# Fifteen blocks of one batch per tile: a retention kernel's loads without blocks of the next batch

## The chip, the cores and the metric

The kernel runs on one core of one Trainium2 chip. The metric is device time in microseconds (us) for one execution. The engines are called by the names that the profile uses: PE is TensorE's matmuls, PEld its weight loads, DVE is VectorE, ACT is ScalarE, POOL is GpSimd, SP is SyncE. SP and POOL issue the DMAs.

## The reference, cut to what matters

A retention layer (attention with a decaying mask and no softmax) over 8 batches, 8 heads, 576 tokens and 64 features per head is followed by a mixer: a low-rank step along the tokens and a two-layer perceptron along the 512 channels.

```python
# retention: q, k, v are (8, 8, 576, 64)
scores = (1 / sqrt(64)) * q @ k.transpose(0, 1, 3, 2)
gamma  = 1 - 2.0 ** (-5.0 - arange(8))
Dmat   = where(rel >= 0, gamma[:, None, None] ** rel, 0.0)   # rel = i - j
x      = (scores * Dmat) @ v                                  # then (8, 576, 512)
# mixer: U (576, 32), V (32, 576), w_ch1 (512, 2048), w_ch2 (2048, 512)
u   = x + (x.T @ U @ V).T          # along the tokens of each batch
out = u + relu(u @ w_ch1) @ w_ch2
```

All inputs and the output are float32. The kernel computes in bfloat16, and the loads that POOL issues convert on the way.

## The kernel before, in words

**Tiles.** The 8 x 576 = 4,608 rows of u are cut into nine tiles of 512 rows (`NT`), `j` = 0 to 8. Each tile is one pass of the perceptron (16 column blocks of the first product, then the second product). A batch of 576 tokens is a little longer than a tile, so tile `j` needs u of batch `j - 1` or earlier and of the first part of batch `j`, and the attention and the low-rank step of batch `j + 1` are done while PE works on tile `j`. u lies in a ring of 16 blocks of 128 rows (`ring["u"]`, and transposed `ring["uT"]`).

**Order.** The order of each engine's instructions is written out in the program. In the loop at line 1352, each tile has a list of steps with a number each, and a step goes into the program ahead of the perceptron's unit of that number. Every engine and every queue takes its instructions in this order.

**The loads.** q, k and v of a batch are each read as five blocks of 128 tokens by 8 heads (`load_block`); 576 is four and a half times 128, so one of the five is a half block (the last one in an even batch, the first in an odd batch). That makes fifteen blocks: twelve whole ones and three halves. POOL issues them. Batches 0 to 2 are read in another way, batch 3 ahead of the loop, and the loop reads batches 4 to 7, which is what the change is about. In tile `j` = 2 to 5, `wait_for_turns(j)` lets POOL wait until u of batch `j` has been transposed, and then POOL issues loads for batch `j + 2`, with `load_for_turns` at line 305: for the pairs of blocks (0, 1), (2, 3) and (4) first q and then k, and after them v. Three sets of k and v buffers (`k_sets`, `v_sets`, by batch modulo 3) and two of q are used in turn.

**Blocks ahead.** The table `ahead = {4: 0, 5: 1, 6: 2, 7: 3}` says how many of the first blocks of k and v of a batch were already read one tile earlier. Behind the loads of batch `j + 2` and the clearing of the unused half blocks (`clear_pads`), tile `j` reads those blocks of batch `j + 3`, with `load_batch` at line 316. So the tiles read:

| tile | blocks of its own batch | blocks of the next batch |
|---|---|---|
| 2 | 15 of batch 4 | k and v block 0 of batch 5 |
| 3 | 13 of batch 5 | k and v blocks 0 and 1 of batch 6 |
| 4 | 11 of batch 6 | k and v blocks 0 to 2 of batch 7 |
| 5 | 9 of batch 7 | none |

**What reads the loads.** In the same tile `j`, SP issues six DMA transposes for batch `j + 2` (`turn_by_dma`, line 478): for each pair of blocks one of q and one of k, into `qT_all` and `kT_all` (for every other batch these are the buffers `qz` and `kvT`). Behind them on SP stand the transposes of u of batch `j + 1` into `uT_t`, and stores of finished output. ACT scales v in eight instructions, one for each head (`scale_head`, line 294), at the end of tile `j`. In tile `j + 1` PE takes all of this: the products of k and v that make the states (`pss`), the scores (`sc`), and the first products of the perceptron for tile `j + 1`, which read `uT_t`.

Of the kernel before, what the change touches and what calls it, by code (L numbers as in the profile page):

```python
# [67 lines left out]
def kernel(  # L68
# [23 lines left out]
    NB = (S + P - 1) // P  # L92
    HALF = S - (NB - 1) * P
    SP = NB * P
    NHP = H // 2
# [13 lines left out]
    def rows_of(b, m):  # L109
        if b % 2 == 0:  # L110
            return (0, HALF) if m == NB - 1 else (0, P)
        return (HALF, P) if m == 0 else (0, P)

    def token_of(b, m):
        return m * P if b % 2 == 0 else m * P - HALF
# [24 lines left out]
    NRUNS = 3  # L140
    NTURN = 3
    NQ = 2
    q_raw = [consts.tile([P, NR_COLS], BF16, name=f"q_all{i}") for i in range(NQ)]
# [8 lines left out]
    def in_runs(x):  # L152
        return x[0:NR, :].rearrange("p (h i d) -> p h i d", h=H, i=RUN)
# [4 lines left out]
    NSET = 3  # L158
    k_sets = [consts.tile([P, NB, H, D], BF16, name=f"k_all{i}") for i in range(NSET)]
    v_sets = [consts.tile([P, NB, H, D], BF16, name=f"v_all{i}") for i in range(NSET)]  # L160
# [47 lines left out]
    def load_block(dst, src, b, m):  # L208
        lo, hi = rows_of(b, m)
        t0 = max(token_of(b, m), 0)  # L210
        pool.dma_start(
            out=dst[lo:hi, m, :, :],
            in_=src[b, :, t0:t0 + hi - lo, :].rearrange("h s d -> s h d"),
        )

    def load_runs(dst, src, b, hp):

        h = slice(2 * hp, 2 * hp + 2)
        pool.dma_start(
            out=dst[:, h, :, :].rearrange("p h i d -> p h (i d)"),  # L220
            in_=src[b, h, :, :].rearrange("h (p i) d -> p h (i d)", i=RUN),
        )
# [71 lines left out]
    def scale_head(b, h):  # L294

        x = v_sets[b % NSET][:, :, h, :]
        act.activation(out=x, in_=x, func=AF.Copy, scale=vs64[:, h:h + 1])


    def clear_pads(b):  # L300
        m, pad = (NB - 1, slice(HALF, P)) if b % 2 == 0 else (0, slice(0, HALF))
        for x in (k_sets, v_sets):
            pool.memset(x[b % NSET][pad, m, :, :], 0.0)

    def load_for_turns(b, first=0):

        for c in range(0, NB, 2):
            pair = range(c, min(c + 2, NB))
            load_q(b, pair)
            for m in pair:  # L310
                if m >= first:
                    load_block(k_sets[b % NSET], k, b, m)
        for m in range(first, NB):
            load_block(v_sets[b % NSET], v, b, m)

    def load_batch(b, blocks=range(NB)):

        if b < NRUNS:
            for hp in range(NHP):
                load_runs(in_runs(q_raw[b % NQ]), q, b, hp)  # L320
            for x, src in ((k_sets, k), (v_sets, v)):
                for m in blocks:
                    load_block(x[b % NSET], src, b, m)
            return
        for m in blocks:
            load_block(k_sets[b % NSET], k, b, m)
            load_block(v_sets[b % NSET], v, b, m)

    def load_q(b, blocks):
        for m in blocks:  # L330
            load_block(in_blocks(q_raw[b % NQ]), q, b, m)

    def wait_for_turns(b):

        for a, n in in_ring(chunks_of(b)):
            pool.tensor_copy(out=landed[:, 0:n], in_=ring["uT"][:, a:a + n, 0, 0])
# [247 lines left out]
    def attention_steps(b, at, gap, at_mixer, at_turn=2):  # L584

        x_t = work.tile([P, NB, dm], BF16, tag="x_t", name="x_t")
        sts = [{} for _ in range(NHP)]
        mst = {}
        steps = []

        for hp in range(NHP):
            if b < NRUNS:
                steps.append((at[hp] - (3 if hp else 1), 4, lambda hp=hp: scale_v(b, hp)))
            steps.append((at[hp], 1, lambda hp=hp: att_transposes(b, hp, sts[hp])))
            steps.append((at[hp] + gap, 2, lambda hp=hp: visit(b, hp, sts, x_t)))
        steps.append((at[NHP], 0, lambda: visit(b, NHP, sts, x_t)))
        steps.append((at_mixer, 0, lambda: mix_middle(b, x_t, mst)))
        steps.append((at_mixer + 2, 0, lambda: mix_up_full(b, x_t, mst)))
        part = (NB - 1) * (1 - b % 2)
        steps.append((at_mixer + (2.5 if b % 2 else 5 if b > 2 else 8), 0, lambda: (  # L600
            mix_up(b, part, x_t, mst))))
        turns = [(a + i, min(2, n - i)) for a, n in in_ring(chunks_of(b)) for i in range(0, n, 2)]
        for i, (a, n) in enumerate(turns):
            steps.append((at_mixer + 3.2 + i, 1, lambda a=a, n=n: mix_turn_by_dma(a, n)))
        if NTURN <= b + 1 < B:
            for i, (src, dst, c) in enumerate(
                    (src, dst, c) for c in range(0, NB, 2)
                    for src, dst in ((in_blocks(q_raw[(b + 1) % NQ]), qT_sets[(b + 1 - NTURN) % 2]),
                                     (k_sets[(b + 1) % NSET], kT_sets[(b + 1 - NTURN) % 2]))):
                steps.append((at_turn + i, 5, lambda src=src, dst=dst, c=c: (  # L610
                    turn_by_dma(src, dst, c))))
        steps.sort(key=lambda s: s[:2])
        return steps
# [308 lines left out]
    def sums_of_w2(part):  # L922

        f = slice(part * HF // 2, (part + 1) * HF // 2)
        (b11, b12), (b21, b22) = (
            [w2_sb[:, fh * HF:(fh + 1) * HF, q * HD:(q + 1) * HD][:, f, :] for q in range(2)]
            for fh in range(2)
        )
        t3, t2, t4 = (w2_sums[:, i, f, :] for i in range(3))
        for to, x, y, op in (  # L930
            (t3, b22, b12, ALU.subtract), (t2, t3, b11, ALU.add), (t4, b21, t2, ALU.subtract),
        ):
            dve.tensor_tensor(out=to, in0=x, in1=y, op=op)

    def last_sum_of_w2(part):
        f = slice(part * HF // 2, (part + 1) * HF // 2)
        x = w2_sb[:, 0:HF, HD:dm][:, f, :]
        dve.tensor_tensor(out=x, in0=x, in1=w2_sb[:, 0:HF, 0:HD][:, f, :], op=ALU.subtract)
# [331 lines left out]
    while n < SP:  # L1270
        m = min(n, SP - n)
# [72 lines left out]
    clear_pads(3)  # L1344
    pool.tensor_copy(out=landed[:, 0:2], in_=kT_sets[1][:, 0:2, 0, 0])
    load_for_turns(3)
    for name, n in (("one", 3), ("two", 1)):
        banks[name] = ctx.enter_context(
# [3 lines left out]
    for j in range(1, NT):  # L1352
        if j == 1:
            clear_pads(4)
        steps = []
        if j == 1:
            steps = sorted(
                attention_steps(2, (5, 8.5, 12, 15.5, 21), 1.5, 22, 8) + late
                + [(at, 3, lambda i=i: sums_of_w2(i)) for i, at in enumerate((3.2, 21.5))],
                key=lambda s: s[:2]  # L1360
            )
        elif j + 1 < B:
            last = 17 if j < 5 else 16
            steps = attention_steps(j + 1, (-1.5, 2.5, 6.5, 10.5, last), 1.5, last + 1.8)
        if j == 2:
            steps += [(at, 3, lambda i=i: last_sum_of_w2(i)) for i, at in enumerate((2, 3))]
        if 1 < j and j + 2 < B:
            ahead = {4: 0, 5: 1, 6: 2, 7: 3}
            wait_for_turns(j)
            load_for_turns(j + 2, ahead[j + 2])  # L1370
            if j + 3 < B:
                clear_pads(j + 3)
                load_batch(j + 3, range(ahead[j + 3]))
        if j + 2 < B:
            at = 22 if j == 1 else 20
            steps += [(at + h, 4, lambda h=h: scale_head(j + 2, h)) for h in range(H)]
        steps.sort(key=lambda s: s[:2])
        for n, unit in enumerate(units1 if j == 1 else mlp_units(j)[0]):
            while steps and steps[0][0] <= n:
                steps.pop(0)[2]()  # L1380
            if j > 1 or n >= 3:
                unit()
        for s in steps:
            s[2]()
# [31 lines left out]
```

## Time and profile before

| what | us |
|---|---|
| median of 3 runs | 318.52 (317.9 to 318.59) |
| the profiled execution's own time | 314.95 |
| its span | 313.2 |
| PE busy in the span | 305.0 |

The span is the part of the profiled execution from its first to its last instruction. "Busy" is the time in which an engine works on instructions. A wait is told by what ended it. DMA transfers of POOL are on queue q0 (software_dynamic), those of SP on queue q1 (hardware_dynamic), and both run on the same 16 DMA engines; a queue's share is given as a share of these 16 engines' time, and it can be over 100% where packets of several queues overlap. Almost all instructions stand under line 25 in the profile, because a helper records them there, so groups are told by the names of their tiles.

### The profile page before, as it was taken

The numbers are of one execution on the slowest core, as the hardware profiler recorded it, in microseconds if no ns is written. First come the engines' busy times: TensorE is split into PE (matmuls) and PEld (weight loads), VectorE is DVE, ScalarE is ACT, GpSimd is POOL, SyncE is SP. The second block draws the span as 40 slices with busy tenths as digits, with TensorE's granted clock in tenths as the row PEclk, the third lists the DMA queues.
The fourth block names the chain that finished last, engine by engine and source line by source line (L and its number), as shares of the span: only waits on it lengthen the run. The fifth ranks groups of instructions, "written<-read, shape, count | busy, mean of one in ns | idle before, by whom it ended". The sixth has DMA issues, their size and how long they took to land.

```text
span 313.2 us, 9448 instructions
## 1 busy us (share of the span) xinstructions
PE 305.0 (97%) x3952; PEld 189.6 (61%) x3952; DVE 228.2 (73%) x562; ACT 167.2 (53%) x346; POOL 131.5 (42%) x171
## 2 busy tenths in 40 slices
PE   8899999999999999999979999999999999999995
PEld 3674456644544558755864578457845784685484
DVE  6967729869988997899686968997799772342244
ACT  7657515357526774477356872678167406604610
POOL 8682349749302973079608922811200120040040
PEclk9999999999999999999999999999999999999999
DMA  7999999999998999999999999999510052002003
GB/s 119 204 203 195 202 206 132 171 174 134 147 139 175 162 115 144 139 168 151 150 157 211 138 134 178 176 148 104 166 37 4 3 138 80 2 33 103 0 2 135
DMA packets 154523, 40.58 MB, mean 130 GB/s; under 512 B 139088, under 2 KB 153456, under 8 KB 154480
## 3 DMA queue, kind: packets, MB, share of 16 engines
q0 software_dynamic: 91344, 17.09, 70.8%
q1 hardware_dynamic: 63136, 22.88, 42.6%
q8 instruction: 31, 0.51, 0.7%
q14 instruction: 12, 0.10, 0.1%
HBM read 36.85 MB, written 9.44 MB: 148 GB/s over the span
## 4 chain that ended last, share of the span: by engine, by line
PE 82%; DMA 6%; DVE 5%; issue 1%; SPq 0%; POOL 0%; DVEq 0%; POOLq 0%
PE ps_y L25 68%; PE xh L25 5%; PE ps_b L25 4%; DMA uT_t<-u_t 3%; DMA y_sums<-in_k_dram 2%; DMA kv_runs<-in_v_dram 2%; PE sc L25 2%; PE ps_h L25 1%; PE pss L25 1%; PE ps_at L25 1%; DVE v_all L25 1%; DVE u_t L25 1%; DVE V_sb L25 1%; DVE qz L25 1%; PE psq L25 0%
## 5 line engine op out<-in xcount | busy, mean ns | idle before, releaser
L25 PE MATMUL ps_y<-uT_t,w_sb 128*128 128x512 bf16 x576 | 130.3, 379 | 1.9 <-DMA uT_t<-u_t 1.9
L25 ACT ACTIVATE y_t<-ps_y 128x512 bf16<-128x512 f32 x144 | 85.7, 597 | 63.7 <-PE ps_y L25 62.6
L25 PEld LDWEIGHTS <-w_sb 128*128 128x128 bf16 x576 | 54.4, 98 | 63.5 <-DMA uT_t<-u_t 2.0
L25 PEld LDWEIGHTS <-y_t 128*128 128x128 bf16 x576 | 55.1, 98 | 18.9
L25 POOL TENSOR_TENSOR o_sb<-o_sb,u_t 128x512 f32<-128x512 f32 x21 | 24.0, 1152 | 101.0 <-DVE o_sb L25 98.0
L25 PE MATMUL ps_y<-w_sb,y_t 128*128 128x256 bf16 (+1 forms) x352 | 57.5, 311 | 0.0
L25 DVE SCALAR_TENSOR_TENSOR S<-S,keep,pss 128x64 bf16<-128x64 bf16 x168 | 47.0, 280 | 5.1
L25 DVE TENSOR_TENSOR o_sb<-ps_y,o_sb 128x512 f32<-128x512 f32 (+1 forms) x37 | 24.4, 662 | 26.3 <-PE ps_y L25 12.8
L25 DVE TENSOR_TENSOR ret<-sc,qsrow 128x640 bf16<-128x640 f32 x48 | 39.3, 819 | 4.9 <-PE sc L25 4.6
L25 PEld LDWEIGHTS <-y_sums 128*128 128x128 bf16 x336 | 32.0, 98 | 4.9 <-issue 0.2
L25 POOL DMA_DIRECT2D k_all<-in_k_dram x36 | 30.2, 849 | 8.8 <-DMA w_sb<-in_moe_w_ch_dram 8.1
L25 POOL DMA_DIRECT2D q_all<-in_q_dram x37 | 29.2, 795 | 5.3 <-DMA w_sb<-in_moe_w_ch_dram 4.1
L25 DVE TENSOR_TENSOR y_sums<-y_t 128x512 bf16<-128x512 bf16 x28 | 11.7, 419 | 22.1 <-ACT y_t L25 22.1
L25 POOL DMA_DIRECT2D v_all<-in_v_dram x31 | 26.7, 896 | 2.2 <-DMA k_all<-in_k_dram 1.4
L25 PE MATMUL ps_y<-w_sb,y_sums 128*128 128x256 bf16 x224 | 27.4, 273 | 0.0
L25 PE MATMUL ps_y<-kv_runs,y_t 128*128 128x256 bf16 x224 | 26.9, 273 | 0.0
L25 ACT ACTIVATE x_t<-xh,xs 128x320 bf16<-128x320 f32 x48 | 22.7, 523 | 7.3 <-PE xh L25 5.5
L25 ACT ACTIVATE v_all<-v_all,vs 128x320 bf16<-128x320 bf16 x40 | 18.7, 548 | 12.5 <-DMA v_all<-in_v_dram 9.4
L25 DVE TENSOR_TENSOR u_t<-ps_h,x_t 128x512 bf16<-128x512 f32 (+2 forms) x39 | 22.3, 628 | 2.5 <-PE ps_h L25 2.3
L25 POOL COPY landed<-uT_t 128x4 bf16<-128x4 bf16 (+3 forms) x5 | 0.9, 188 | 41.8 <-DMA uT_t<-u_t 41.8
L25 ACT CAST S<-pss 128x64 bf16<-128x64 f32 x24 | 5.0, 208 | 17.7 <-issue 16.7
L25 PE MATMUL ps_y<-kv_runs,y_sums 128*128 128x256 bf16 x112 | 14.1, 273 | 0.0
(134 smaller groups left out, 303.0 us busy)
## 6 DMA issues: line engine op xcount, KB each, us to landing
out_dram<-o_sb SPq DMA_DIRECT2D x35, 256.0 KB, 2.5
w_sb<-in_moe_w_ch_dram POOLq DMA_DIRECT2D x8, 512.0 KB, 10.8
v_all<-in_v_dram POOLq DMA_DIRECT2D x25, 128.0 KB, 9.8
k_all<-in_k_dram POOLq DMA_DIRECT2D x24, 128.0 KB, 7.0
q_all<-in_q_dram POOLq DMA_DIRECT2D x20, 128.0 KB, 4.6
q_all<-in_q_dram POOLq DMA_DIRECT2D x12, 144.0 KB, 6.8
given<-in_v_dram SPq DMA_DIRECT2D x8, 128.0 KB, 5.2
kv_runs<-in_v_dram SPq DMA_DIRECT2D x3, 256.0 KB, 6.0
```

Source lines behind the costliest of these rows:

```text
L25: return self._tc.keep_in_program_order(call(*args, **kwargs))
```

## The change

Each of the tiles 2 to 5 reads all fifteen blocks of one batch, and no block of the batch after it. `load_for_turns` loses its parameter `first`. `load_batch` loses its parameter `blocks` and the branch for later batches, since only batch 2 still uses it. The table `ahead` and the call that read ahead go. The order inside `load_for_turns`, the transposes, the scaling of v and everything else stay.

```diff
-    def load_for_turns(b, first=0):
+    def load_for_turns(b):
 
         for c in range(0, NB, 2):
             pair = range(c, min(c + 2, NB))
             load_q(b, pair)
             for m in pair:
-                if m >= first:
-                    load_block(k_sets[b % NSET], k, b, m)
-        for m in range(first, NB):
+                load_block(k_sets[b % NSET], k, b, m)
+        for m in range(NB):
             load_block(v_sets[b % NSET], v, b, m)
...
         if 1 < j and j + 2 < B:
-            ahead = {4: 0, 5: 1, 6: 2, 7: 3}
             wait_for_turns(j)
-            load_for_turns(j + 2, ahead[j + 2])
+            load_for_turns(j + 2)
             if j + 3 < B:
                 clear_pads(j + 3)
-                load_batch(j + 3, range(ahead[j + 3]))
```

More of the change, by code (lines that the diff above doesn't have):

```diff
@@ L310, in load_for_turns, with load_batch @@
             for m in pair:
-                if m >= first:
-                    load_block(k_sets[b % NSET], k, b, m)
-        for m in range(first, NB):
+                load_block(k_sets[b % NSET], k, b, m)
+        for m in range(NB):
             load_block(v_sets[b % NSET], v, b, m)
[L316 to L327, printed above, removed]
+    def load_batch(b):
+        for hp in range(NHP):
+            load_runs(in_runs(q_raw[b % NQ]), q, b, hp)
+        for x, src in ((k_sets, k), (v_sets, v)):
+            for m in range(NB):
+                load_block(x[b % NSET], src, b, m)
     def load_q(b, blocks):
```

## The prediction

> **What bounds the kernel now.** I read the page first: the busy line, the slices of TensorE (PE) and of DMA.
>
> ```profile
> span 313.2 us, 9448 instructions
> ...
> PE 305.0 (97%) x3952; PEld 189.6 (61%) x3952; DVE 228.2 (73%) x562; ACT 167.2 (53%) x346; POOL 131.5 (42%) x171
> ...
> PE   8899999999999999999979999999999999999995
> ...
> DMA  7999999999998999999999999999510052002003
> ```
>
> PE works almost without a gap. Its one 7 after the start is the slice at 157 to 164 us (each is 7.8 us). DMA is full until about 219 us and nearly idle from 227 on: the loads are over. So the change, which only moves loads, can act on the time only where PE waits for a transfer. The waits of PE from 95 us on are one row (in total, times, longest), and the chain in order of time shows its place (start, us, what):
>
> ```profile
> PE ps_y L25 <- DMA uT_t<-u_t: 1.9, 1, 1.9
> ```
>
> ```profile
> 156.36 7.86 DMA uT_t<-u_t
> 164.27 3.63 PE ps_y L25 x16
> ```
>
> Tile 4 cannot start before the first DMA transpose of batch 4's u has landed; it is issued at 156.36, lands at 164.22, and PE has been out of work for 1.9 us. The row of the windows for tile 3 (stage, its length, PE busy, the other engines, clock, DMA) says the same, 33.07 us with PE busy for 31.21, at the full clock of 1.00:
>
> ```profile
> 131.20:164.27 33.07, 31.21 (x466) 20.49 (x462) 27.86 (x63) 19.36 (x42) 19.26 (x23) 1.00 1.65 150
> ```
>
> **How much moves.** All loads concerned are on q0, the queue that POOL fills. Its packets in the windows of tiles 2, 3, 4 and 5 (99 to 131, 131 to 164, 164 to 196, 196 to 227 us), and last those of 104 to 107 us, when it had the engines to itself:
>
> ```profile
> q0 software_dynamic: 15120, 1.90, 96.3%
> ...
> q0 software_dynamic: 17168, 2.16, 108.7%
> ...
> q0 software_dynamic: 15120, 1.90, 108.5%
> ...
> q0 software_dynamic: 8848, 1.11, 61.4%
> ...
> q0 software_dynamic: 3485, 0.44, 229.8%
> ```
>
> The code explains the four: a batch has 12 whole blocks and 3 half ones, 13.5 in all. Tile 2 loads 14.5 (a half k and a half v block of batch 5 beside batch 4), tile 3 loads 16.5, tile 4 loads 14.5, tile 5 only 8.5. After the change each loads 13.5, a quarter of the 56,256 packets: 14,064. Tiles 2 and 4 lose 1,056 packets each, tile 3 loses 3,104, tile 5 gains 5,216. Alone, q0 moves 3,485 / 3 = 1,162 packets a us, so that is 0.9, 2.7, 0.9 us less and 4.5 us more of DMA time. No DMA is added or removed, sixty loads stay sixty, and the transposes and stores on SP keep their order.
>
> What delays the transposes is seen at 152 to 155 us, when both queues have work:
>
> ```profile
> q0 software_dynamic: 1256, 0.16, 80.3%
> q1 hardware_dynamic: 1258, 0.31, 80.3%
> ```
>
> They get the same number of packets, so a load that is not there gives its time to the transposes on q1.
>
> At this place the Trainium skill has a price of its own: the page "DMA: Bandwidth & Descriptors", section "Anatomy of one DMA — SWDGE (gpsimd) path", gives a transfer's variable part as bytes / 436 GB/s. By it 3,104 packets (0.39 MB) would be an estimated 0.9 us, and tile 3 would keep 1.0 us of its stall; the row above, with packets of 126 bytes, gives 2.7 us, and the row decides.
>
> **The clocks that matter.** I time each tile from its first load. The rows are those of POOL's first loads for tiles 2 to 5, then SP's issues (start, time on SP's queue), then the landings of the first five of these in the same order, each the first issue of its row (us from issue to landing, the last number):
>
> ```profile
> 99.68 1.75 POOL L25 DMA_DIRECT2D q_all<-in_q_dram  x2 [0.33 <-PE ps_y L25]
> ...
> 135.21 1.60 POOL L25 DMA_DIRECT2D q_all<-in_q_dram  x2 [0.27 <-issue]
> ...
> 165.64 3.54 POOL L25 DMA_DIRECT2D q_all<-in_q_dram  x4 [0.27 <-issue]
> ...
> 197.27 3.42 POOL L25 DMA_DIRECT2D q_all<-in_q_dram  x4 [0.27 <-issue]
> ```
>
> ```profile
> 120.03 2.32 SPq L25 DMA_TRANSPOSE kvT<-k_all  x1
> 126.15 2.54 SPq L25 DMA_TRANSPOSE uT_t<-u_t  x2
> ...
> 153.44 1.22 SPq L25 DMA_TRANSPOSE kT_all<-k_all  x1
> ...
> 190.19 3.43 SPq L25 DMA_TRANSPOSE uT_t<-u_t  x2
> ...
> 215.28 1.22 SPq L25 DMA_TRANSPOSE kT_all<-k_all  x1
> 220.27 2.59 SPq L25 DMA_TRANSPOSE uT_t<-u_t  x2
> ```
>
> ```profile
> kvT<-k_all SPq DMA_TRANSPOSE x1, 8.0
> ...
> uT_t<-u_t SPq DMA_TRANSPOSE x1, 2.7
> ...
> kT_all<-k_all SPq DMA_TRANSPOSE x1, 8.0
> ...
> uT_t<-u_t SPq DMA_TRANSPOSE x1, 4.1
> ...
> kT_all<-k_all SPq DMA_TRANSPOSE x1, 4.0
> ```
>
> The last transpose of k lands 28.4 us after the first load in tile 2 (128.0), 26.2 in tile 3 (161.4), 22.0 in tile 5 (219.3). The first of u follows 0.9 us behind it in tile 2 (128.9) and 2.8 in tile 3 (164.2, so 29.0 after the first load); in tile 4 it lands at 194.3, 28.7 after. PE would take it, had it no wait, right after the last score matmuls or at the rows of tiles 5 and 6:
>
> ```profile
> 162.07 0.33 PE L25 MATMUL sc<-qT_all,kT_all 64*64 64x64 bf16 x20
> ...
> 195.44 3.63 PE L25 MATMUL ps_y<-uT_t,w_sb 128*128 128x512 bf16 x16
> ...
> 226.80 3.63 PE L25 MATMUL ps_y<-uT_t,w_sb 128*128 128x512 bf16 x16
> ```
>
> That is at 162.4, 195.4 and 226.8, or 27.2, 29.8 and 29.5 us after the first load of tiles 3, 4 and 5. Tile 3 has the least room, and today the most packets.
>
> **Part by part.** *Tile 2* becomes lighter by 0.9 us. PE waited for nothing there, and the first load of tile 3 follows its own u transposes, so I count nothing (0 to 0.9 earlier).
>
> *Tile 3* is the gain. Its four loads for batch 6 go, its two for batch 5 come in. The last of those four are still running when the transposes end, so of the 2.7 us I count 1.9 to 2.7. Against this stands the order: k's first block is no longer there before, so one load of 0.9 us (1.75 / 2) goes ahead of what the first k transpose waits for. SP is a queue in order, and behind that transpose stand the other four, the u transposes and the stores; but q0's packets run meanwhile, so 0 to 0.9 of it is lost. The u transpose then lands 26.3 to 28.0 us after the first load, against 27.2: a stall of 0 to 0.8, middle 0.
>
> The second thing to be late is ScalarE (ACT). Its eight scalings of v wait for the last v block, and the next tile's first state copy and its eviction stand behind them:
>
> ```profile
> 124.58 3.73 ACT L25 ACTIVATE v_all<-v_all,vs 128x320 bf16<-128x320 bf16 x8 [2.99 <-POOL o_sb L25]
> 157.39 3.73 ACT L25 ACTIVATE v_all<-v_all,vs 128x320 bf16<-128x320 bf16 x8 [4.62 <-DMA v_all<-in_v_dram]
> 163.44 2.17 DVE L25 SCALAR_TENSOR_TENSOR S<-S,keep,pss 128x64 bf16<-128x64 bf16 x7
> ```
>
> VectorE (DVE) begins to add up the states at 163.44, 1.0 us after PE is ready; for that v must have landed 3.73 us of scaling and a small state copy (some 0.2) earlier, 2.9 us before PE is ready: 159.5, 192.5 and 223.9 in the three tiles. In tile 3 v's last block goes from 12.5 to 13.5 blocks deep, 0.9 us at the rate alone to 2.5 at the shared 419 a us: 158.3 to 159.9, so 0 to 0.4 late. Of the 1.9 us I therefore let 0.4 stay: **-1.5 us** (ends: -1.9, and -0.7 if the two upper ends add up).
>
> *Tile 4* gets 0.9 us lighter, and its first two k blocks, so far loaded by tile 3, come behind the first two of q: up to 0.9 later again. Its u transpose lands 27.8 to 28.7 after the first load, against 29.8. Cost 0. Its v, whole in this tile as in tile 2, lands as there by 24.9 us (124.58), at 190.5, against 192.5.
>
> *Tile 5* takes six more loads, 4.5 us. What covers them are the 7.5 us that today lie between 219.3, when the last k transpose is in, and 226.80, less what u's own landing takes of them. The last k transpose goes to 26.5 after the first load, u's to 27.4 to 29.3, against 29.5: cost 0. Three k blocks that were there already have to be waited for, which the pairwise order of q and k limits as in tile 4. By tile 2's 24.9, v lands at 222.2 against 223.9. POOL's three additions of the tile stand behind the loads in its queue; fifteen issues of 0.9 us end some 13 us after the first, long before v's landing. Without that cover each late us is a us of the end, since nothing after 227 us has slack for it.
>
> Sum: -1.5. On the profiled execution that is 314.95 to 313.45 us (span 313.2 to 311.7). The runs shown have their median 3.57 us above that execution (318.52); no trace shows where these lie, and I take the same difference: **317.0 us**.
>
> **The rivals.** *Slower: tile 2's pace holds everywhere.* Tile 2 alone already loads its whole batch itself, and its last k transpose lands 2.2 us later from the first load than tile 3's, although tile 3 loads two blocks more. If that is the price of waiting for one's own k, then each tile gets 28.4 - 0.9 = 27.5, and with tile 3's 2.8 behind it u lands at 30.3: stalls of 3.1, 0.5 and 0.8 in tiles 3, 4 and 5, 4.4 against 1.9 now. That is +2.5, 321.0 us. It decides against the change from 29.1 us on (27.2 + 1.9). For it speaks that one tile, the only one with this order; against it that u followed after 0.9 there and not 2.8, and that the two are added here although they stood in different tiles. The Trainium skill speaks for this side: "DMA: Bandwidth & Descriptors", section "Rules for kernel authors", says to issue a DMA early and to wait for it late, which is what the ahead blocks do; the profile shows a DMA without a free slice there, where earlier means ahead of something else.
>
> *A wash.* Tile 2's pace with a gap of 0.9 to 2.0: u lands at 28.4 to 29.5, so a stall of 1.2 to 2.3 in tile 3 takes the place of the 1.9, and there is none elsewhere. That is -0.7 to +0.4; as a number, from the middle, 318.4.
>
> *More than forecast.* If the 3.57 us of the timed runs are the same kind of wait, all three lighter tiles pay: 0.9 + 2.7 + 0.9 less 1.5 for tile 5 is -3.0, 315.5 us.
>
> *The change does not do what it says* is out: the built order of POOL's queue has all fifteen loads of each batch in one piece.
>
> **How the numbers follow.** Forecast 0.38, more than forecast 0.10, the wash 0.19 (nearly all of it within the bound), slower 0.33. What a measurement of this kernel can tell from no change is 0.2%, 0.64 us. So faster 0.48, within 0.18, slower 0.34. The range goes from the third rival to the slower one: 315.5 to 321.0 us, with about 0.2 outside, mostly a slower case with more than one wait in a tile. The faster cases alone span 315.5 to 317.8.
>
> **What would show it.** Right: PE's wait for u at the start of tile 4 under 0.8 us, no new one at tiles 5 and 6; q0 near 14,064 packets in each of the four windows; DMA's slices busy to the end of tile 5. Wrong: PE waiting for u's transposes or for the state sums at the start of tiles 5 or 6; a u transpose later than 29.1 us after tile 3's first load; ACT's scalings of v in tile 5 later than 223.9 us.

## The result, and the profile after

The changed kernel took 314.32 us (median of 7 runs, 313.67 to 315.51); the kernel before, run again beside it, 317.48 (7 runs, 316.34 to 318.59). The ratio is 0.9905, with a 95% interval of 0.9876 to 0.9935: 3.0 us less, twice the 1.5 us of the forecast, and below the forecast's range. Later runs on other chips gave ratios of 0.9986 (0.9954 to 1.0019) and 0.9966 (0.9924 to 1.0007), and both intervals take in 1. These ratios leave out executions that are over 1.5% above the fastest of their kernel, and here that takes out many of the kernel before and almost none of the changed one, so I also give medians of all executions: over all whose granted clock is known, on several chips, 317.1 us (124 executions of the kernel before) against 315.1 us (31 of the changed one), 2.0 us less.

The page of the changed kernel, whose profiled execution took 315.51 us; the rows are the span, and in 40 slices PE's busy tenths, the granted clock and DMA's busy tenths:

```profile
span 313.8 us, 9434 instructions
...
PE   8799999999999999999999999999999999999995
...
PEclk9979999999999999999999999999999999999999
DMA  7999999999995999799999994999910052002003
```

The 7 among PE's slices at 157 to 164 us is gone, and DMA is busy one slice longer, to about 227 us. The 7 in the clock's line, at 16 to 23 us, is a stretch at half the granted clock that the profile of before does not have; it lies in the beginning, where the two kernels are the same, and tile 2 starts 1.5 us later (at 101.3 us, not 99.9), which more than makes up for the gain in this one pair of profiles (313.8 us against 313.2).

q0's packets, in the stretches from the start of tile 2 to that of tile 6 (100 to 132.64, to 163.83, to 195.65, to 227.28 us):

```profile
q0 software_dynamic: 14064, 1.77, 90.5%
...
q0 software_dynamic: 14064, 1.77, 93.3%
...
q0 software_dynamic: 14064, 1.77, 97.5%
...
q0 software_dynamic: 14064, 1.77, 95.6%
```

The first loads of tile 3, the transposes of u at its end, with the landing of the first, and PE's one wait from 95 us on:

```profile
136.75 1.60 POOL L25 DMA_DIRECT2D q_all<-in_q_dram  x2 [0.27 <-issue]
```

```profile
157.86 3.85 SPq L25 DMA_TRANSPOSE uT_t<-u_t  x2
```

```profile
uT_t<-u_t SPq DMA_TRANSPOSE x1, 4.9
```

```profile
PE ps_y L25 <- issue: 0.3, 1, 0.3
```

u lands at 162.7, and PE needs it at 163.8. The wait of 1.9 us is gone. The transpose is issued as long after tile 3's first load as before (21.1 us in both profiles), but it lands 4.9 us after its issue and not 7.9. The packets of q0 in the 4 us behind this issue, in the kernel before (156.4 to 160.4 us) and in the changed one (157.9 to 161.9), show why:

```profile
q0 software_dynamic: 2046, 0.26, 115.3%
...
q0 software_dynamic: 118, 0.01, 5.5%
```

What the list of waits does not show stands in the windows of tiles 3, 4 and 5 (from first product to first product; stage, length, PE busy, then the other engines):

```profile
132.64:163.83 31.19, 31.14 (x469) 20.50 (x462) 26.06 (x59) 17.53 (x38) 17.38 (x22) 1.00 1.54 158
163.83:195.65 31.82, 31.67 (x472) 20.74 (x462) 26.28 (x59) 20.68 (x45) 17.02 (x20) 1.00 1.52 152
195.65:227.28 31.63, 31.28 (x472) 20.50 (x462) 26.14 (x59) 17.88 (x39) 16.23 (x19) 1.00 1.66 158
```

Tile 3 has come from 33.1 us to 31.2, which is its length without any wait. Tile 4 has grown from 31.2 to 31.8.

### The profile page after: what moved, and what is told of

It reads as the page before. It is cut to its first block, busy times and chain, and to the rows that moved or that the text cites. A ratio compares the mean times of both kernels' runs of the same rounds, so it can differ in the third digit from the quotient of the medians.

```text
span 313.8 us, 9434 instructions
## 1 busy us (share of the span) xinstructions
PE 305.6 (97%) x3937; PEld 190.9 (61%) x3952; DVE 229.0 (73%) x562; ACT 166.8 (53%) x346; POOL 131.3 (42%) x171
## 4 chain that ended last, share of the span: by engine, by line
PE 84%; DVE 7%; DMA 4%; issue 2%; SPq 1%; ACT 0%; POOL 0%; DVEq 0%; POOLq 0%
PE ps_y L25 69%; PE xh L25 5%; PE ps_b L25 4%; DMA given<-in_v_dram 2%; DMA kv_runs<-in_v_dram 2%; PE sc L25 2%; SPq L25 1%; PE pss L25 1%; DVE u_t L25 1%; PE ps_h L25 1%; PE ps_at L25 1%; DVE v_all L25 1%; DVE S L25 1%; DVE V_sb L25 1%; DVE qT_all L25 1%
## 5 line engine op out<-in xcount | busy, mean ns | idle before, releaser
L25 POOL TENSOR_TENSOR o_sb<-o_sb,u_t 128x512 f32<-128x512 f32 x21 | 23.9, 1152 | 104.8 <-DVE o_sb L25 100.3
L25 PE MATMUL ps_y<-w_sb,y_t 128*128 128x256 bf16 (+1 forms) x345 | 56.4, 310 | 0.5 <-issue 0.2
L25 DVE TENSOR_TENSOR o_sb<-ps_y,o_sb 128x512 f32<-128x512 f32 (+1 forms) x37 | 24.4, 662 | 26.6 <-PE ps_y L25 12.8
L25 POOL DMA_DIRECT2D v_all<-in_v_dram x31 | 26.5, 918 | 2.4 <-DMA k_all<-in_k_dram 1.6
L25 PEld LDWEIGHTS <-ret 128*128 128x128 bf16 (+1 forms) x320 | 11.8, 98 | 2.5 <-issue 0.2
```

Of the source, the lines that this page charges most:

```text
L25: return self._tc.keep_in_program_order(call(*args, **kwargs))
```

## The experiments

Two tables hold what the runs gave; the sections after them say what was done and what follows. First the times. "Low clock" counts the executions with a mean granted clock under 0.997, wherever in the execution the clock was lowered; the column beside it is the kernel before, run beside it on the same chip.

| run | median us (n) | low clock | before: median (n), low clock | ratio, 95% interval |
|---|---|---|---|---|
| b_again | 316.51 (12) | 4 | 316.88 (31), 16 | 1.0028, 0.9991 to 1.0066 |
| a_again | 315.13 (12) | 1 | as above | 0.9986, 0.9954 to 1.0019 |
| t3_light | 314.88 (12) | 2 | as above | 0.9975, 0.9940 to 1.0010 |
| after_4_twice | 318.39 (8) | 7 | as above | 1.0103, 1.0065 to 1.0141 |
| b_filled | 316.78 (12) | 4 | 317.74 (23), 17 | 1.0007, 0.9970 to 1.0045 |
| a_pool67 | 314.05 (12) | 2 | as above | 0.9906, 0.9874 to 0.9937 |
| a_third | 315.14 (12) | 3 | 317.56 (35), 17 | 0.9966, 0.9924 to 1.0007 |
| a_pool67_2 | 313.59 (12) | 1 | as above | 0.9931, 0.9898 to 0.9965 |
| b_pool67 | 317.36 (12) | 7 | as above | 1.0020, 0.9976 to 1.0064 |
| t5_heavy | 316.95 (12) | 7 | as above | 1.0046, 1.0007 to 1.0085 |
| after_4_twice_2 | 318.27 (11) | 9 | 317.11 (21), 13 | 1.0064, 1.0034 to 1.0095 |
| after_4_twice_filled | 318.25 (11) | 4 | as above | 1.0025, 0.9988 to 1.0061 |

Some of these times were not what was expected. The ratios of a_again (expected 0.988 to 0.994) and t3_light (0.990 to 0.995) are nearer to 1, that of after_4_twice (0.998 to 1.004) is higher, and the two filled kernels lost neither as much time nor as many executions with a low clock as expected.

Second the profiles: where tile 2 starts, the lengths of tiles 3, 4 and 5, each from its first product to that of the next tile, PE's wait ahead of tile 4, and where the granted clock was halved for 3.4 us.

| profile | tile 2 starts | tile 3 | tile 4 | tile 5 | wait | half clock at |
|---|---|---|---|---|---|---|
| before, as shown | 99.9 | 33.1 | 31.2 | 31.4 | 1.9 | none |
| b_again | 101.1 | 32.8 | 31.2 | 31.2 | 1.6 | none |
| b_fourth | 101.3 | 33.4 | 31.2 | 31.2 | 2.2 | none |
| b_third | 99.2 | 34.5 | 32.7 | 31.2 | 3.3 | 164.8 |
| t5_heavy | 100.0 | 33.8 | 31.2 | 31.3 | 2.4 | none |
| b_pool67 | 100.0 | 35.1 | 32.8 | 31.2 | 2.5 | 166.4 |
| b_filled | 102.2 | 33.9 | 31.2 | 31.2 | filled, 0.6 left | 15.1 |
| after | 101.3 | 31.2 | 31.8 | 31.6 | none | 16.0 |
| a_again | 101.1 | 31.2 | 32.3 | 31.2 | none | none |
| a_third | 100.2 | 31.2 | 31.3 | 31.2 | none | none |
| a_pool67 | 102.5 | 31.2 | 31.2 | 31.2 | none | none |
| a_pool67_2 | 100.1 | 31.2 | 31.2 | 31.2 | none | none |
| t3_light | 101.4 | 31.2 | 32.1 | 31.2 | none | none |
| after_4_twice | 100.3 | 34.1 | 32.5 | 31.8 | 2.9 | 165.1 |
| after_4_twice_2 | 101.5 | 34.7 | 32.9 | 31.2 | 3.4 | 167.6 |
| after_4_twice_filled | 99.2 | 34.0 | 31.2 | 31.2 | filled | none |

No edit touches what stands ahead of tile 2, yet tile 2 starts between 99.2 and 102.5 us. Tile 2 itself takes 31.2 to 31.3 us in every profile, and from the start of tile 6 to the end of the span they all take 86.4 to 86.5 us.

**Both kernels again** (b_again, a_again: no edit).

> The kernel before, unchanged, timed and profiled anew. Theory (the gain is the wait of PE for u's transpose at the start of tile 4, and in most executions that wait is longer than the 1.9 us of the profile shown): the profile shows this wait at 3 to 4.5 us and nearly no other wait behind 95 us, with the span 1 to 3 us over 313.2. Rival (all three lighter tiles pay): the wait at tile 4 stays at 1.9 us and others of 0.5 to 1 us stand at the starts of tiles 3 and 5. Rival (the shown execution was short at its beginning): tile 2 begins later than at 99.9 us by 1 to 3 us and the wait at tile 4 is 1.9 us. Ratio 1.000.

> The changed kernel, unchanged, timed and profiled anew. Theory: ratio 0.988 to 0.994; from the start of tile 2 to the start of tile 5 93.8 us plus at most 0.7 us of waits, against that plus 1.9 or more in the kernel before. Rivals: the same ratio; by the second also the stretches of tiles 2 and 4 are shorter than before's by 0.5 us each, by the third the stretch from tile 2 to tile 5 differs by no more than 1.9 us.

My theory in that form fell for this profile of the kernel before: its wait was 1.6 us, shorter than in the first, and there is a small one of 0.9 us just ahead of tile 2. What fits this profile is the rival that the shown execution was short at its beginning: tile 2 starts 1.2 us later than in the first profile, and tiles 3 to 5 are 0.5 us shorter. The list of waits:

```profile
PE ps_y L25 <- DMA uT_t<-u_t: 1.6, 1, 1.6
PE sc L25 <- ACT uT_t L25: 0.9, 1, 0.9
```

But its times on this chip, 313.9 to 319.8 us for one and the same kernel, fall in two groups by the granted clock: over all its executions 68 of 124 are under 0.997, with a median of 318.4 us, and the others have 315.4. Of the changed kernel's 31, 5 are under it. In a_again the stretch from tile 2 to tile 5 is 94.8 us, 1.0 over 93.8 and not the 0.7 allowed, and 0.8 under the first profile of the kernel before, as the same rival allows; tile 4 took 32.3 us of it, without a wait in the list. The next three rows say why (start, length, idle time before and what ended it), with PE's row behind them:

```profile
161.97 3.73 ACT L25 ACTIVATE v_all<-v_all,vs 128x320 bf16<-128x320 bf16 x8 [7.95 <-DMA v_all<-in_v_dram]
...
165.72 0.21 ACT L25 CAST S<-pss 128x64 bf16<-128x64 f32 x1
...
165.96 2.18 DVE L25 SCALAR_TENSOR_TENSOR S<-S,keep,pss 128x64 bf16<-128x64 bf16 x7 [1.20 <-ACT S L25]
...
167.43 0.98 PE L25 MATMUL xh<-S,qT_all 64*64 64x64 bf16 x16
```

v's last block lands at 161.9, ACT scales until 165.7, only then copies the first state, and DVE, idle for 1.2 us, ends the states when PE already needs them. The sixteen products `xh` take 0.98 us where they take 0.32 elsewhere: PE's wait is inside its busy time.

**Tile 3 alone lighter** (t3_light).

```diff
-            ahead = {4: 0, 5: 1, 6: 2, 7: 3}
+            ahead = {4: 0, 5: 1, 6: 0, 7: 3}
```

> The table of blocks ahead becomes 4: 0, 5: 1, 6: 0, 7: 3: tile 3 reads nothing of batch 6, tile 4 reads all of batch 6 and the blocks of batch 7 as before. In blocks the tiles 2 to 5 load 14.5, 12.5, 18.5, 8.5. Theory (tile 3's load is what costs): the wait at the start of tile 4 goes, ratio 0.990 to 0.995, unless tile 4 with 18.5 blocks gets a wait of its own at the start of tile 5; that one would be 0 to 2.5 us, since tile 4 had 1.1 us of room with 14.5. Rival (all three lighter tiles pay): tile 4's wait takes back all of it, ratio 0.998 to 1.005.

Tile 3 without its four extra loads loses its wait, and the median is that of the changed kernel (314.88 against 315.13). Tile 4, with 18.5 blocks, has a wait at its end, but only a short one:

```profile
PE ps_y L25 <- DMA uT_t<-u_t: 0.8, 1, 0.8
```

So it is tile 3's amount that pays. Tile 4 had more room than the clocks of the prediction gave it: 1.1 us of room against four blocks of 0.9 us should have left some 2.5 us.

**The changed kernel with tile 3 one block heavier than before** (after_4_twice: 17.5 blocks; the kernel before has 16.5).

```diff
                 clear_pads(j + 3)
+                if j == 3:
+                    for m in range(2):
+                        load_block(k_sets[6 % NSET], k, 6, m)
+                        load_block(v_sets[6 % NSET], v, 6, m)
```

> The changed kernel, but tile 3 reads the first two k and v blocks of batch 6 behind its own loads, as before, and tile 4 reads them again: tile 3 loads 17.5 blocks and the other tiles 13.5 each. Theory (the amount that tile 3 loads is what costs): the wait at the start of tile 4 comes back with 1.9 to 4 us, ratio to the kernel before 0.998 to 1.004. Rival (what costs is the order, k and v being there early or late): no wait, ratio as the changed kernel's, 0.990.

The wait is back with 2.9 us, and the kernel is slower than the one before. The order of the changed kernel is no help, so with t3_light the amount is shown to be the cause. And the profile has something new: right behind the wait the clock is halved for 3.4 us.

**Two more profiles of the kernel before** (b_third, b_fourth: no edit), to see whether it does that too.

> The kernel before, unchanged, for one more profile. Theory: with a granted clock of 0.995 or lower the half-clock stretch of 3.4 us lies right behind the wait at tile 4's start, and tile 4 is 1.7 us longer than 31.2; with a granted clock of 1.000 there is no such stretch, and the wait is 1.5 to 1.9 us. Rival: the half-clock stretch lies elsewhere.

> One more profile of the kernel before, unchanged. Each theory expects of it what it expects of the run before this one.

b_fourth waited 2.2 us at the full clock, 0.3 more than expected. b_third, with a granted clock of 0.994, has it. Its clock slices, and the row of PE's first products of tile 4:

```profile
PEclk9999999999999999999998999999999999999999
```

```profile
165.03 1.46 PE L25 MATMUL ps_y<-uT_t,w_sb 128*128 128x512 bf16 x3 [3.26 <-DVE S L25]
```

Windows over the wait, the 3.2 us after it, and the whole tile 4 (the clock is the third number from the right):

```profile
161.77:165.03 3.26, 0.00 (x2) 0.00 (x1) 3.05 (x10) 1.00 (x3) 0.00 (x0) 0.97 1.44 164
165.03:168.20 3.17, 3.17 (x8) 1.18 (x9) 0.71 (x1) 0.60 (x1) 1.89 (x3) 0.50 1.04 351
...
165.03:197.77 32.74, 32.74 (x462) 20.89 (x462) 23.15 (x50) 19.00 (x40) 18.53 (x23) 0.95 1.59 162
```

PE does nothing for 3.26 us, then only eight products in 3.17 us at a clock of 0.50, and tile 4 takes 32.74 us in place of 31.17: the stretch costs 1.57 us on top of the wait. (The row names DVE's state sums as what ended the wait, at 165.01, but these products read only u and the weights, and u's transpose landed at 164.99. In after_4_twice the list names DVE as well, with u landing at 165.7 and the product at 165.77; in the other profiles it names the transpose.)

The Trainium skill has this: "TensorE: Matmul & The Clock Gate", section "HAM oscillation — how this bites in real kernels", says to leave PE no idle gaps over some 3.4 us, since the clock is then halved. The halved clock agrees, 0.50 here; the length of the gap does not quite: waits of 1.6, 1.9, 2.2 and 2.4 us kept the clock, and waits of 2.5, 2.9, 3.3 and 3.4 lost it (the one of 2.5 had another of 1.2 us just before it). The length of one wait alone does not decide: in after_4_twice the clock fell 2.2 us into the wait, while t5_heavy's wait of 2.4 us kept it.

**PE kept busy during the wait** (b_filled: nine extra products in the kernel before; after_4_twice_filled: thirteen in after_4_twice, beside after_4_twice_2, which is after_4_twice again). The extra products write a constant into the bank that tile 4's first product then starts anew.

```diff
             held[f] = ps = ps_mm.tile([P, 512], FP32, tag="mm", name="ps_y1")
+            if j == 4 and f == order[0]:
+                for _ in range(9):                      # 13 in after_4_twice_filled
+                    pe.matmul(
+                        ps.rearrange("p (a b) -> p a b", a=4), warm,
+                        warm[:, None, :].to_broadcast([P, 4, P]), start=True, stop=True,
+                    )
```

> The kernel before, with nine extra products of a constant tile (128x512 each, 1.9 us in all) on PE ahead of tile 4's first product, into the bank that this product then starts anew: PE works while it waits for u's transpose, and the wait itself is not shortened. Theory now (a wait of PE at tile 4 of 1.6 to 3 us is followed in about half of the executions by 3.4 us at half the granted clock, which adds some 1.7 us or more to the wait): executions with a granted clock under 0.997 fall from 20 of 43 to under 1 in 5, and the median falls from 316.9 to 315.5 us, ratio of all runs about 0.995. Rival (the lower clock comes from elsewhere and has nothing to do with the wait): the share of executions with the lower clock stays near half, and the median stays at 316.9 us or above.

> The changed kernel with tile 3 reading the first two k and v blocks of batch 6 as well (tile 4 reads them again), unchanged, beside the next run on the same chip. Theory: a wait for u's transpose of 2.5 to 4 us at tile 4's start, a granted clock under 0.997 in at least 5 of 8 executions, median 318.4 us, 1 to 1.5 us over the kernel before.

> The same kernel, with thirteen extra products of a constant tile (2.8 us) on PE ahead of tile 4's first product, so that PE works through most of the wait; loads and transposes are untouched. Theory (the half-clock stretch comes from PE being without work for about 2.5 us or more): executions with a granted clock under 0.997 fall to 2 of 8 or fewer, what is left comes from the first 20 us, and the median falls by 1.0 to 1.6 us against the run beside it. Rival (the stretch comes from the time of the execution or from the load of the chip, and not from the idle PE): the share stays, the median stays or rises.

The share of executions with the lower clock fell both times, from 17 of 23 to 4 of 12 and, in the kernel with the doubled loads, from 16 of 19 (9 of 11 in the executions beside it) to 4 of 11, but not to the 1 in 5 and 2 of 8 that were expected. The first of these says little by itself, since the kernel before without filling also had 4 of 12 once, in b_again. The profiles are clearer: without filling, 3.4 us of PE without work are followed by half the clock, with filling they are not. b_filled's profile has its lowered clock in the beginning, behind 3.1 us in which PE worked for 1.01, and none behind the filled wait.

```profile
164.09:167.52 3.43, 0.00 (x1) 0.01 (x1) 2.22 (x6) 2.16 (x6) 0.00 (x0) 1.00 1.47 164
167.60:171.00 3.40, 3.40 (x9) 1.19 (x10) 1.55 (x4) 0.60 (x1) 1.72 (x3) 0.50 1.10 320
```

```profile
161.72 2.98 PE L25 MATMUL ps_y<-warm 128*128 128x512 bf16 x13
164.54 3.62 PE L25 MATMUL ps_y<-uT_t,w_sb 128*128 128x512 bf16 x16
```

```profile
12.00:15.10 3.10, 1.01 (x33) 1.00 1.21 203
15.10:18.50 3.40, 3.40 (x66) 0.50 0.63 80
```

The first two rows are after_4_twice_2 (the wait, then the stretch), the next two after_4_twice_filled, the last two the beginning of b_filled (length, PE busy, clock, DMA). Tiles 3 to 5 together take 96.3 us in the filled profile against 98.7. The times did not follow as expected: the filled kernel's median is 318.25 against 318.27, and b_filled's is 1.0 us below the kernel before with no difference in the ratio. That PE's idling halves the clock is shown by the profiles; that this alone is worth 1.6 us is shown in profiles only, and the measured times do not show it. The filled kernel's executions at the full clock spread from 315.0 to 318.4 us. The beginning is one place where executions differ: tile 2 starts at 99.2 us in after_4_twice_filled and at 101.5 in after_4_twice_2, which is 2.3 of the 4.7 us between these two. None of the longer filled executions was profiled, so where they lose their time stays open.

**What comes late in its place** (a_pool67, a_pool67_2: the changed kernel, POOL scales two of v's eight heads; b_pool67: the same in the kernel before).

```diff
         x = v_sets[b % NSET][:, :, h, :]
+        if h in (6, 7) and b > 4:
+            pool.tensor_tensor(
+                out=x, in0=x, in1=vs64[:, h:h + 1, None].to_broadcast([P, NB, D]), op=ALU.mult
+            )
+            return
         act.activation(out=x, in_=x, func=AF.Copy, scale=vs64[:, h:h + 1])
```

> The changed kernel, but POOL scales the last two heads of v for batches 5 to 7 in place of ACT (ACT six scalings, 2.8 us, POOL two behind its additions). Theory (in the changed kernel, tile 4 starts with v's scaling as what ends last: 1.0 us of the gain is lost there): ACT is free 0.9 us earlier at the start of tile 4, tile 4 from its first product to tile 5's goes from 31.8 to 32.3 us down to 31.2 to 31.6, and the median from 315.1 to 314.2 us. Rival (POOL's wait for v holds up its loads for the next tile): the first load of tile 4 comes 1 us later or more, tile 5 starts no earlier, median 315.1 us or above.

> The changed kernel once more, on the same chip as the three runs beside it. Theory (the change takes away a wait of 1.6 to 3.3 us at tile 4's start, and with it the half-clock stretch behind the longer of these waits; about 1 us comes back as ACT's late scaling of v): against the kernel before 1.5 to 3 us less in the medians, and at most 3 of 12 executions with a granted clock under 0.997, against about half or more of the kernel before.

> The changed kernel with the last two heads of v for batches 5 to 7 scaled by POOL, once more and beside the changed kernel on one chip. Theory (ACT's scaling of v is what comes late in its place): 0.7 to 1.2 us under the changed kernel's median, a ratio of 0.996 to 0.998 between them. Rival (the first comparison mixed two chips): no difference over 0.3 us.

> The kernel before, with the last two heads of v for batches 5 to 7 scaled by POOL. Theory (in the kernel before, u's transpose ends last at tile 4's start, 1 us or more behind v's scaling): no gain, the ratio of the medians 0.998 to 1.002, and the wait for u's transpose of 1.5 to 3.3 us still there. Rival (v's scaling holds up the kernel before as well, at other places): 0.9 us less, ratio 0.997.

On one chip the changed kernel had a median of 315.14 and this version 313.59, 1.5 us less (expected 0.7 to 1.2); in both comparisons it lies 3.7 to 4.0 us under the kernel before. It is the fastest version of this study. The profiles show only a part of the 1.5 us: tile 4 lost 0.6 us to v in the mean of the changed kernel's three, and a_third lost just 0.15 there, so that tiles 3 to 5 take 93.7 us in it and 93.6 in a_pool67_2. In the kernel before, the same edit changes nothing (317.36 against 317.56), and the wait for u is still there, behind one of 1.2 us for k's transpose that no other profile has. Its list of waits:

```profile
PE ps_y L25 <- DMA uT_t<-u_t: 2.5, 1, 2.5
PE sc L25 <- DMA kT_all<-k_all: 1.2, 1, 1.2
```

ACT's rows at the start of tile 4 in a_pool67_2, and the windows of its tiles 3, 4 and 5:

```profile
160.86 2.82 ACT L25 ACTIVATE v_all<-v_all,vs 128x320 bf16<-128x320 bf16 x6 [7.80 <-DMA v_all<-in_v_dram]
163.71 0.21 ACT L25 CAST S<-pss 128x64 bf16<-128x64 f32 x1
```

```profile
131.43:162.62 31.19, 31.14 (x469) 20.50 (x462) 26.12 (x59) 17.23 (x37) 18.59 (x23) 1.00 1.61 154
162.62:193.84 31.22, 31.17 (x471) 20.55 (x461) 26.34 (x59) 19.27 (x42) 18.62 (x23) 1.00 1.69 153
193.84:225.01 31.17, 31.12 (x471) 20.50 (x462) 26.13 (x59) 18.05 (x39) 17.65 (x21) 1.00 1.68 167
```

Six scalings take 2.82 us in place of 3.73, the state copy starts 1.1 us after tile 4's first product and not 2.2 after it as in a_again, and all three tiles are at their length without waits. POOL's wait for v did not hold up its loads: the first of tile 4 comes 0.7 us after tile 4's first product, and in a_again 1.0.

**Tile 5 heavy, tile 3 as before** (t5_heavy).

```diff
-            ahead = {4: 0, 5: 1, 6: 2, 7: 3}
+            ahead = {4: 0, 5: 1, 6: 2, 7: 0}
```

> The table of blocks ahead becomes 4: 0, 5: 1, 6: 2, 7: 0: tiles 2 and 3 load as before (14.5 and 16.5 blocks), tile 4 loads 9.5 and tile 5 all 13.5 of batch 7. Theory (tile 3's amount is what costs, and tile 5 has room for its own fifteen blocks but for ACT's scaling of v, some 0 to 0.5 us late there): the wait at tile 4's start stays at 1.5 to 3.3 us, a granted clock under 0.997 in about half of the executions, the median within 0.6 us of the kernel before. Rival (the balance of all four tiles is what pays): 0.9 us less from tile 4.

The median is 0.6 us less (316.95 against 317.56), the ratio 0.5% more, so there is no gain that both show. The wait at tile 4's start stayed:

```profile
PE ps_y L25 <- DMA uT_t<-u_t: 2.4, 1, 2.4
```

Tile 5 takes its fifteen blocks with no wait (31.3 us). Tile 4 is lighter by 5 blocks and no shorter, 31.2 us as in the kernel before: there was nothing to gain in it.

## Why the prediction was right and wrong

**Right: where and why.** Only tile 3's load mattered, and it acted through the u transpose ahead of tile 4: t3_light and after_4_twice take the wait away and bring it back with the amount. From its issue to its landing this transpose takes 7.9, 7.6, 9.3 and 8.2 us in the four profiles of the kernel before, 4.9, 5.6 and 4.9 in the three of the changed one, 3.9 in t3_light and 8.9 in after_4_twice. The packets are 14,064 in each tile, to the packet. The u transpose was forecast 26.3 to 28.0 us after tile 3's first load; it lands 26.0 us after in the first profile (162.7 from a first load at 136.75) and 26.5 in the other two. The new order of k, for which up to 0.9 us was allowed, cost nothing: the transpose is issued no later than before. Tiles 2, 4 and 5 cost and gained nothing in PE's waits, as forecast, but for 0.3 us of unknown cause inside tile 5 in one of three profiles.

**Right, but too small: v's scaling.** That ACT's scaling would be late in u's place was named, with at most 0.4 us. v was to land 23.1 to 24.7 us after tile 3's first load; ACT started 25.3 us after it in a_again (161.97 from 136.71), and tile 4 lost 0.65, 1.1 and 0.15 us in the three profiles, 0.6 in the mean. The bound of 24.7 came from the 419 packets a us of one short stretch; why v lands later than that is not shown. In tile 5 ACT's scaling started 26.6 to 27.8 us after the first load, not by 24.9, and in two of the three profiles it started after 223.9 us, which the prediction had named as a sign of being wrong. It cost at most 0.1 us, in tile 6.

**Wrong: the size of the gain.** The step that failed is the term for what goes away: the 1.9 us of one execution were taken as the wait, 0.4 of them were let stay, and the 3.57 us between that execution and the median were carried over whole, as if none of them belonged to this wait. In other executions of the kernel before the wait is 1.6, 2.2 and 3.3 us, and behind the longest PE's clock is halved, which costs 1.57 us more. The changed kernel has no such wait, and 5 of 31 of its executions have a lowered clock, against 68 of 124. From the tables: tiles 3 to 5 take 95.7, 95.2, 95.8 and 98.4 us in the four profiles of the kernel before, 96.2 in the mean, and 94.6, 94.7 and 93.7 in the three of the changed kernel, 94.3 in the mean. That is 1.9 us where 1.5 was forecast, and the medians of all executions differ by 2.0.

Three things temper this. The forecast time of 317.0 us stood on a median of three runs, 318.52; seven gave 317.48, and that is 1.0 of the 2.7 us between the forecast and the result. The 3.57 us were not this wait alone: 16 of 124 executions were shorter than the one shown, and the three other profiled ones were 0.6, 2.1 and 1.5 us longer, of which the beginning, the same in both kernels, makes 1.2, -0.6 and 1.4 us, and tiles 3 to 5 make -0.5, 2.8 and 0.1. And the agreement of 1.9 and 2.0 is partly luck. Among the executions at a clock of 0.997 or more the medians are 315.4 and 315.1 us, only 0.3 apart, while the three full-clock profiles of the kernel before lose 1.2 us more in tiles 3 to 5 than the changed kernel's three. So most of the measured gain lies in the share of executions with a lowered clock; what takes back the rest at the full clock is open, and so is why the first comparison gave 3.0 us and the later ones less.

**The rivals.** "More than forecast" had -3.0, the number of the first comparison (all executions together give 2.0), but for another reason: it let tiles 2 and 4 pay. Tile 2 takes the same 31.2 to 31.3 us in every profile, and t5_heavy rules tile 4 out. The slower rival fell at its deciding point: u at 26.0 us, and not beyond 29.1. The rule that spoke for it, to issue early and to wait late (the Trainium skill, "DMA: Bandwidth & Descriptors", section "Rules for kernel authors"), did not hold in tile 3, because the early loads took time from a transpose that was wanted sooner. The wash, with u at 28.4 to 29.5, fell at the same point.

## What to carry to other kernels

Where DMA is full, count each stage's packets against the time at which the stage's last transfer is needed, and level the load to the stage with the least room; reading ahead only moves packets in front of something else. Price a wait of PE from several executions, and add what the clock loses behind it. If one profiled execution is some us faster than the median of the timed runs, find out what the others do before forecasting from it, and find out in which part of the program they do it. When a wait goes, look at what stood 1 us behind it: here ACT's scaling, which was worth another 1.5 us in the medians.

## What was not expected of the hardware

The granted clock is lost at waits of PE that are shorter than I had thought: at 2.5 to 3.4 us, for 3.4 us at 0.50, and in one profile 2.2 us into the wait. A PE wait can also hide in PE's busy time: sixteen small products were busy for 0.98 us instead of 0.32 while they waited for their operands, and the list of waits had nothing.
